# Cumulated sums of the first pair of heads: spread over the partitions by transposes on TensorE, and an exponential ahead

## The chip, the cores and the metric

The kernel runs on one core of a Trainium2 chip. The metric is the time of the device in microseconds (us): the median of three runs before the change is 1105.16 us (1102.88 to 1105.53).

## The reference

Three stages, all in float32 (the weights come as float64 and are converted on the chip):

```python
# q, k, v: (4 batches, 8 heads, 576 positions, 64); f: (4, 8, 576)
scores = q @ k.T / sqrt(64)
cum = cumsum(log(clip(f, 0.0001, 1)), axis=-1)
scores = where(above_diagonal, -1e9, scores + cum[..., :, None] - cum[..., None, :])
attn = softmax(scores) @ v                      # row maximum subtracted first
x = attn as (2304 tokens, 512)
h = x @ w_in; y = max(0.01 * h, h) @ w_out      # 512 -> 2048 -> 512
out = ((y @ w_a) * (y @ w_b)) @ w_o2            # 512 -> 1536 -> 512
```

The term `cum[query] - cum[key]` is the one that the change touches. For a tile with queries on the partitions and keys along the free axis, `cum[query]` is one number per partition, but `cum[key]` is a row that every partition needs: it has to be spread over all 128 partitions.

## The kernel before

The kernel is written in a tile framework. The source says for each instruction which engine it runs on; a planner with its own estimate of every duration then lays out the order on each engine and in each queue, by readiness and priority, and inserts all waits. Priorities: instructions of attention are issued through wrappers (`pe_att`, `act_att`, `dve_att`, `pool_att`) that put them 300 places ahead of others. Each engine works through its instructions strictly in that order. All loads are issued by SP, one queue, in order.

The work is cut into attention blocks (batch b, half r of the queries): block (0, 0) has queries and keys 0 to 255, block (0, 1) the other queries with all keys. A block takes its 8 heads in pairs. For each head `att_scores` makes scores (s, TensorE, into PSUM), the decay tile p (GpSimd: row of sums of the keys, less the sum of the query, then the causal mask by an affine select), adds both and takes the row minimum (VectorE, L330 and its like) and takes the exponential with the row sum (ScalarE, L301). `att_values` transposes p on TensorE (pp), copies it out of PSUM (ph) and multiplies with v (av); a last transpose (px) gives xh, the input of the first dense stage. For batch 0 many instructions show line 76, that of the wrappers.

Beside block (0, 0), and beside the following ones, the weights come in: `fetch_weight` (L115) loads 1 MB of float64 in two requests (raw_a from w_in and from w_out), `convert_weight` turns them into two float32 parts with ScalarE (L94, L87) and VectorE (L95, L96, L97, L100, L88). Weight 1 stands in the order as written, each weight from the third on waits for the beginning of the conversion two before it. The first dense product h (L590) needs all four pairs of block (0, 0) and the first two weights. It is taken 2000 places ahead.

The sums are made at the start (L151 to L166): f is loaded with 32 partitions (one per batch and head), clipped (L152), Ln on ScalarE (L153), a scan on VectorE gives cum (L157), which is written to DRAM as cum_dram (L158). TensorE transposes cum (pc, L162), and ScalarE writes it negated as `ncum_t` (L163) and `ncum_t4` (L165, L166): positions on the partitions, one column per head. In block (0, 0) each pair of heads has a tile cumb of 128 x 2 x 256; it is filled by two DMAs that read a row of cum_dram and repeat it over 128 partitions (L293). In the other blocks each head has its own (L297). The tiles fs, cum and cumb share three slots.

Of the kernel before, what the change touches and what calls it, by code (L numbers as in the profile page):

```python
# [8 lines left out]
F32 = mybir.dt.float32  # L9
# [3 lines left out]
AF = mybir.ActivationFunctionType  # L13
# [4 lines left out]
P = 128  # L18
# [8 lines left out]
def kernel(  # L27
# [13 lines left out]
    nc = tc.nc  # L41
    B, H, S, D = q.shape
# [12 lines left out]
    cum_dram = dram.tile([B * H, S], F32, name="cum_dram")  # L55
# [4 lines left out]
    ident = cpool.tile([P, P], F32, name="ident")  # L60
    make_identity(nc, ident)
    ncum_t = cpool.tile([P, 4, B * H], F32, name="ncum_t")
    ncum_t4 = cpool.tile([P, B * HP], F32, name="ncum_t4")
# [83 lines left out]
    ps_a = att_ctx.enter_context(tc.tile_pool(name="ps_att", bufs=1, space=PSUM, side="right"))  # L147


    fs = ap_.tile([B * H, S], F32, tag="cumb", bufs=3, name="fs")  # L150
    nc.sync.dma_start(fs, f.rearrange("b h s -> (b h) s"))  # L151
    nc.vector.tensor_scalar(fs, fs, 0.0001, 1.0, op0=ALU.max, op1=ALU.min)  # L152
    nc.scalar.activation(fs, fs, AF.Ln)  # L153
    ones = ap_.tile([B * H, S], F32, tag="tk", name="ones")
    nc.vector.memset(ones, 1.0)
    cum = ap_.tile([B * H, S], F32, tag="cumb", bufs=3, name="cum")
# [21 lines left out]
    x4, p4s, stats, qks, xns, vhls, phs, cums, lasts, lastk = ({} for _ in range(10))  # L178

    def att_scores(b, r, h, st):  # L180

        hp, j = h // 2, h % 2
        bh = b * H + h
# [3 lines left out]
        nk = 2 * P if r == 0 else S  # L187
# [101 lines left out]
        if first:  # L289
            if j == 0:  # L290
                cums[hp] = ap_.tile([P, 2, 2 * P], F32, tag="cumb", bufs=3, name=f"cumb_{nm}")
                for u in range(2):
                    nc.sync.dma_start(cums[hp][:, u, :], cum_dram[bh + u : bh + u + 1, :nk].to_broadcast([P, nk]))  # L293
            cumb = cums[hp][:, j, :]
        else:
            cumb = ap_.tile([P, S], F32, tag="cumb", bufs=3, name=f"cumb_{nm}")
            nc.sync.dma_start(cumb[:, :nk], cum_dram[bh : bh + 1, :nk].to_broadcast([P, nk]))  # L297
# [12 lines left out]
        ps = st["ps"] = {}  # L310
        for i in range(2):
            t = 2 * r + i
# [407 lines left out]
    def att_steps(n):  # L720

        if n == 0:

            sts = [{} for _ in range(H)]
            scores = [att_scores(*blocks[n], h, sts[h]) for h in range(H)]
            values = [att_values(*blocks[n], h, sts[h]) for h in range(H)]
            before = None
            for h in range(0, 2):
                next(scores[h])
            for h in range(0, H, 2):  # L730
                for z, _ in enumerate(beside(beside(*scores[h : h + 2]), before)):
                    if z == 3:
                        for g in scores[h + 2 : h + 4]:
                            next(g)
                    yield
                before = chain(*values[h : h + 2])
            yield from before
            return
        second = None
        for h in range(H):  # L740
            st = {}
            yield from beside(att_scores(*blocks[n], h, st), second)
            second = att_values(*blocks[n], h, st)
            if h % 2 == 1 and blocks[n][1] == 1:
                second = chain(second, att_last(blocks[n][0], h // 2, st["rec4"]))
        yield from second
# [143 lines left out]
```

## Time and profile before

| | us |
|---|---|
| median of three runs (lowest, highest) | 1105.16 (1102.88, 1105.53) |
| the profiled execution | 1102.89 |
| its span, first to last instruction | 1101.1 |
| TensorE busy | 1079.5 (98%) |
| VectorE, ScalarE, GpSimd busy | 590.4, 536.7, 224.7 |
| mean granted TensorE clock | 0.992 of full |

The profile shows one execution. PE is TensorE, PEld its loading of weights, DVE is VectorE, ACT is ScalarE, POOL is GpSimd, SPq the queue from which SP issues DMAs. Times are us from the span's start.

### The profile page before, as it was taken

How to read it: one execution, taken by the hardware profiler on the slowest of the kernel's cores; microseconds unless marked ns; L12 is line 12 of the kernel's file. 1: busy time of each engine (PE TensorE's matmuls, PEld its weight loads, DVE VectorE, ACT ScalarE, POOL GpSimd, SP SyncE). 2: the span in 40 equal slices, each digit the busy share in tenths (PEclk: the TensorE clock that was granted, in tenths of full speed). 3: DMA queues.
4: the chain of work that ended last, by engine and by line, in shares of the span. 5: the costliest groups of instructions: out<-in, count | busy, mean ns of one | idle time of the engine just before them, and what ended most of it. 6: DMA issues, size and time to landing. Idle time of an engine off the chain costs nothing.

```text
span 1101.1 us, 19263 instructions
## 1 busy us (share of the span) xinstructions
PE 1079.5 (98%) x7021; PEld 967.4 (88%) x7021; DVE 590.4 (54%) x1314; ACT 536.7 (49%) x1189; POOL 224.7 (20%) x434
## 2 busy tenths in 40 slices
PE   4999999999999999999999999999999999999998
PEld 2768889999999999999999998888888888888897
DVE  5978846787778787677447889212111211211122
ACT  5666657777788777778534565112112111211121
POOL 4734512433233432433000000202001000100000
PEclk9979999999999999999999999999999999999999
DMA  8967225432354233521026562102000100100010
GB/s 232 273 197 203 43 40 107 91 89 47 73 115 81 73 75 74 135 52 48 4 94 195 198 213 93 48 1 77 1 1 20 48 1 1 48 1 1 1 39 20
DMA packets 185727, 86.76 MB, mean 79 GB/s; under 512 B 143840, under 2 KB 173536, under 8 KB 185632
## 3 DMA queue, kind: packets, MB, share of 16 engines
q1 hardware_dynamic: 180736, 80.80, 28.0%
q10 hardware_dynamic: 4896, 4.72, 1.3%
q8 instruction: 56, 0.92, 0.3%
q14 instruction: 39, 0.32, 0.1%
HBM read 75.96 MB, written 9.51 MB: 78 GB/s over the span
## 4 chain that ended last, share of the span: by engine, by line
PE 90%; DMA 4%; issue 1%; DVE 1%; SPq 1%; ACT 1%; POOL 1%; POOLq 0%; DVEq 0%; ACTq 0%
PE ab L686 27%; PE h L590 17%; PE y L617 17%; PE o L709 13%; PE av L76 6%; PE s L76 6%; PE pp L76 4%; DMA raw_a<-in_moe_w_out_dram 1%; DMA cumb<-cum_dram 1%; POOL p L347 0%; DMA vn<-in_v_dram 0%; DMA cum_dram<-cum 0%; DMA xk<-in_k_dram 0%; POOL p L324 0%; SPq L115 0%
## 5 line engine op out<-in xcount | busy, mean ns | idle before, releaser
L686 PE MATMUL ab<-yh,w_ab 128*128 128x512 f32 (+1 forms) x960 | 279.5, 367 | 0.0
L590 PE MATMUL h<-xh,w_a 128*128 128x256 f32 x1152 | 226.9, 283 | 0.5 <-ACT hs L600 0.5
L617 PE MATMUL y<-gh,w_a 128*128 128x256 f32 x1152 | 223.7, 282 | 0.0
L686 PEld LDWEIGHTS ab<-yh,w_ab 128*128 128x128 f32 x960 | 174.2, 188 | 30.4
L692 DVE TENSOR_TENSOR p<-ab,p 128x512 f32<-128x512 f32 (+1 forms) x60 | 38.3, 638 | 285.8 <-PE ab L686 285.8
L590 PEld LDWEIGHTS h<-xh,w_a 128*128 128x128 f32 x1152 | 184.5, 189 | 3.8 <-issue 2.1
L617 PEld LDWEIGHTS y<-gh,w_a 128*128 128x128 f32 x1152 | 182.5, 188 | 2.4 <-issue 1.3
L686 PE MATMUL ab<-yl,w_ab 128*128 128x512 f32 (+1 forms) x480 | 176.2, 367 | 0.0
L590 PE MATMUL h<-xl,w_a 128*128 128x256 f32 x576 | 163.2, 283 | 0.0
L617 PE MATMUL y<-gl,w_a 128*128 128x256 f32 x576 | 161.1, 281 | 0.0
L709 PE MATMUL o<-w_c,pph 128*128 128x512 f32 x432 | 142.5, 389 | 0.0
L691 ACT COPY p<-ab 128x512 f32<-128x512 f32 (+1 forms) x60 | 32.7, 544 | 174.3 <-PE ab L686 174.3
L323 POOL TENSOR_SCALAR p<-cumb,ncum_t 128x384 f32<-128x384 f32 (+1 forms) x112 | 82.8, 747 | 139.7 <-PE pp L76 47.0
L590 PEld LDWEIGHTS h<-xl,w_a 128*128 128x128 f32 x576 | 109.0, 189 | 2.4 <-issue 2.0
L617 PEld LDWEIGHTS y<-gl,w_a 128*128 128x128 f32 x576 | 108.3, 188 | 1.1 <-issue 0.8
L686 PEld LDWEIGHTS ab<-yl,w_ab 128*128 128x128 f32 x480 | 90.1, 188 | 15.3
L88 POOL TENSOR_TENSOR yl<-sy,yh 128x512 fp32r<-128x512 f32 (+1 forms) x16 | 20.0, 1261 | 389.2 <-ACT yh L87 389.0
L87 ACT CAST pph<-p 128x512 fp32r<-128x512 f32 (+1 forms) x60 | 34.6, 578 | 128.4 <-DVE p L692 127.8
L301 ACT ACTIVATE p<-p,stat 128x384 f32<-128x384 f32 (+4 forms) x128 | 76.9, 601 | 39.7 <-DVE stat L330 31.2
L709 PEld LDWEIGHTS o<-w_c,pph 128*128 128x128 f32 x432 | 81.1, 188 | 16.6
L709 PE MATMUL o<-w_c,ppl 128*128 128x512 f32 x216 | 84.2, 390 | 0.0
L602 DVE TENSOR_TENSOR gl<-hs,gh 128x512 fp32r<-128x512 f32 x72 | 51.1, 709 | 40.3 <-ACT hs L600 40.1
(140 smaller groups left out, 1756.9 us busy)
## 6 DMA issues: line engine op xcount, KB each, us to landing
cumb<-cum_dram SPq DMA_DIRECT2D x32, 288.0 KB, 3.7
raw_a<-in_moe_w_in_dram SPq DMA_DIRECT2D x16, 512.0 KB, 4.6
raw_a<-in_moe_w_out_dram SPq DMA_DIRECT2D x16, 512.0 KB, 5.7
raw_ab<-in_moe_w_a_dram SPq DMA_DIRECT2D x12, 512.0 KB, 5.1
raw_ab<-in_moe_w_b_dram SPq DMA_DIRECT2D x12, 512.0 KB, 6.1
raw_c<-in_moe_w_out_dram SPq DMA_DIRECT2D x12, 512.0 KB, 5.7
xq<-in_q_dram SPq DMA_DIRECT2D x144, 32.0 KB, 2.1
y_dram<-yo ACTq DMA_DIRECT2D x18, 256.0 KB, 2.5
```

The costliest lines, as they stand in the source:

```text
L76: return method(*args, **kw)
L87: nc.scalar.copy(hi, src)
L88: (lo_engine or nc.gpsimd).tensor_tensor(out=lo, in0=src, in1=f32(hi), op=ALU.subtract)
L301: act_att.activation(pt, pt, AF.Exp, bias=stat[:, 0, s : s + 1], scale=-1.0, accum_out=stat[:, 1, s : s + 1])
L323: pool_att.tensor_scalar(pt, cumb[:, :n], 1.0, ncum_t[:, t, bh : bh + 1], op0=ALU.mult, op1=ALU.add)
L590: nc.tensor.matmul(hps[:, u, :], w[:, c * P : c * P + P], x[:, c, :], start=(n == 0), stop=(n == 3 * ND - 1))
L602: nc.vector.tensor_tensor(out=gl, in0=hs, in1=f32(gh), op=ALU.subtract)
L617: nc.tensor.matmul(o, w[:, d * P : d * P + P], g[:, u, :], start=(fi == 0 and n == 0 and d % 2 == 0), stop=(fi == NF1 - 1 and n == 2 and d ...
L686: nc.tensor.matmul(o[:, :tn], w[:, c * P : c * P + P], y[:, c, :tn], start=(m == 0), stop=(m == 3 * ND - 1))
L691: nc.scalar.copy(p[:, :tn], ab[0][:, :tn])
L692: nc.vector.tensor_tensor(out=p[:, :tn], in0=ab[1][:, :tn], in1=p[:, :tn], op=ALU.mult)
L709: nc.tensor.matmul(o, g[:, t * P : t * P + P], w, start=(fi == 0 and m == 0), stop=(fi == NF2 - 1 and m == 2))
```

## The change

Two edits. An exponential of one column is issued behind the Ln; its result goes to a place that L165 overwrites later. And in block (0, 0) the first pair of heads no longer fills its cumb by DMA: for each of the two heads and of the two tiles of 128 keys, the column of `ncum_t` is taken as a 128x128 operand that repeats it, and a transpose puts it as a row on all 128 partitions of a PSUM tile rep (128 x 512 in all); ScalarE copies that, times -1, to cumb. cum_dram is written as before, and the other three pairs and all other blocks read it as before. `nc.tensor` and `nc.scalar` are the engines without the 300 places of the wrappers.

```diff
@@ -151,6 +151,7 @@
     nc.scalar.activation(fs, fs, AF.Ln)
+    nc.scalar.activation(ncum_t4[0 : B * H, 0:1], fs[:, 0:1], AF.Exp)
     ones = ap_.tile([B * H, S], F32, tag="tk", name="ones")
@@ -289,8 +290,15 @@
         if first:
             if j == 0:
                 cums[hp] = ap_.tile([P, 2, 2 * P], F32, tag="cumb", bufs=3, name=f"cumb_{nm}")
-                for u in range(2):
-                    nc.sync.dma_start(cums[hp][:, u, :], cum_dram[bh + u : bh + u + 1, :nk].to_broadcast([P, nk]))
+                if hp == 0:
+                    rep = ps_a.tile([P, 2, 2, P], F32, tag="ps", bufs=3, name="rep")
+                    for u in range(2):
+                        for t in range(2):
+                            nc.tensor.transpose(rep[:, u, t, :], ncum_t[:, t, bh + u : bh + u + 1].to_broadcast([P, P]), ident)
+                    nc.scalar.mul(cums[hp], rep.rearrange("p u t k -> p u (t k)"), -1.0)
+                else:
+                    for u in range(2):
+                        nc.sync.dma_start(cums[hp][:, u, :], cum_dram[bh + u : bh + u + 1, :nk].to_broadcast([P, nk]))
             cumb = cums[hp][:, j, :]
```

## Rows read from the trace of the kernel before

**Rows 1.** Busy time by stretch: stretch, us; PE, PEld, DVE, ACT, POOL; clock, DMA, GB/s.
```profile
0.00:25.00 25.00, 11.01 (x35) 6.01 (x35) 13.89 (x27) 12.24 (x26) 9.98 (x24) 1.00 0.78 220
16.00:20.00 4.00, 2.33 (x6) 1.00 (x4) 1.27 (x5) 2.07 (x4) 3.77 (x11) 1.00 1.05 392
25.00:61.00 36.00, 34.45 (x126) 24.12 (x125) 35.83 (x77) 25.13 (x52) 27.60 (x32) 0.90 0.93 268
54.50:70.90 16.40, 15.09 (x46) 8.79 (x46) 13.14 (x27) 9.68 (x19) 5.85 (x7) 0.50 0.83 232
61.00:68.60 7.60, 6.42 (x16) 2.82 (x15) 4.38 (x11) 2.96 (x7) 0.98 (x2) 0.50 0.86 249
72.00:1101.00 1029.00, 1024.17 (x6831) 931.10 (x6830) 533.64 (x1199) 494.23 (x1101) 183.89 (x376) 1.00 0.26 67
```

**Rows 2.** The chain of waits, 5 to 19 us: start, us, what.
```profile
5.36 3.98 DMA cum_dram<-cum
...
11.64 7.28 DMA raw_a<-in_moe_w_out_dram
```

**Rows 3.** Timeline, 3 to 17 us: start, us, instruction, count, idle of its engine before.
```profile
3.27 0.68 ACT L153 ACTIVATE fs<-fs 32x576 f32<-32x576 f32 x1 [1.25 <-DVE fs L152]
4.95 0.38 ACT L76 ACTIVATE qn<-tqk 128x256 f32<-128x256 f32 x1 [0.99 <-PE tqk L76]
6.01 0.69 PE L76 MATMUL tqk<-ident,xk 128*128 128x128 f32 x2
6.12 0.28 ACT L163 ACTIVATE ncum_t<-pc 128x128 f32<-128x128 f32 x1 [0.78 <-PE pc L162]
7.29 0.80 PE L76 MATMUL s<-kn,qn 64*128 64x128 f32 x4 [0.59 <-DVE kn L76]
8.83 1.12 ACT L94 ACTIVATE c_a<-raw_a 128x1024 f32<-128x1024 f32 x1 [2.19 <-DMA raw_a<-in_moe_w_out_dram]
12.43 2.32 POOL L76 TENSOR_SCALAR p<-cumb,ncum_t 128x128 f32<-128x128 f32 x3 [11.11 <-DMA cumb<-cum_dram]
15.29 1.28 ACT L76 ACT_TABLE_LOAD   x1
16.59 0.40 ACT L76 ACTIVATE p<-p,stat 128x128 f32<-128x128 f32 x1
```

**Rows 4.** Prices: PE's group, 29 to 32 us; a page's group; POOL's tiles (min/median/max ns).
```profile
L76 PE MATMUL pp<-ident,p 128*128 128x128 f32 x6 | 1.5, 421 | 0.0
L691 ACT COPY p<-ab 128x512 f32<-128x512 f32 (+1 forms) x60 | 32.7, 544 | 174.3 <-PE ab L686 174.3
L76 POOL TENSOR_SCALAR p<-cumb,ncum_t x12: 370/478/2048, 12.4 to 27.9; 128x128 f32<-128x128 f32 x6, 128x256 f32<-128x256 f32 x6
L76 POOL TENSOR_SCALAR_AFFINE_SELECT p<-p x8: 291/292/294, 14.7 to 19.5; 128x128 f32<-128x128 f32 x8
```

**Rows 5.** Timeline of VectorE, 9 to 15 us: the first of five instructions and the last.
```profile
9.98 0.69 DVE L95 TENSOR_SCALAR c_a<-c_a 128x1024 f32<-128x1024 f32 x1 [2.75 <-ACT c_a L94]
...
12.92 1.22 DVE L100 SCALAR_TENSOR_TENSOR c_a<-raw_a,c_a 128x1024 int32<-128x1024 int32 x1
```

**Rows 6.** Timeline of SP's queue, 9 to 18 us.
```profile
9.36 1.76 SPq L293 DMA_DIRECT2D cumb<-cum_dram  x4
11.17 0.42 SPq L115 DMA_DIRECT2D raw_a<-in_moe_w_in_dram  x1
...
15.88 2.09 SPq L293 DMA_DIRECT2D cumb<-cum_dram  x2
```

**Rows 7.** Groups of VectorE, 20 to 30 us: count, busy us, mean ns, idle before.
```profile
L76 DVE CUSTOM_DVE_ANT_0 p<-s,p 128x256 f32<-128x256 f32 x3 | 1.2, 414 | 0.0
...
L76 DVE CUSTOM_DVE_ANT_0 p<-s,p 128x128 f32<-128x128 f32 x2 | 0.5, 284 | 0.0
L76 DVE DVE_READ_ACCUMULATOR2_ANT stat<- 128x1 f32 x5 | 0.4, 81 | 0.0
L76 DVE TENSOR_SCALAR rec<-stat 128x4 f32<-128x4 f32 x1 | 0.4, 372 | 0.0
```

## The prediction

> **What bounds the kernel now.** I read the busy time by stretch first, then the chain of waits, then the timelines of the first 25 us. From 72 us to the end TensorE is busy for 1024.17 of 1029 us [rows 1]: whatever comes there earlier moves the end one for one. In the first 25 us it is busy for 11.01 us only, so 14.0 us are idle, three times what is left behind 72 us (4.83). The question is how much sooner the front, ahead of 72 us, hands over.
>
> The front has another pace-maker. Between 25 and 61 us VectorE is busy for 35.83 of 36 us, the DMA engines for 0.93 of the time [rows 1]: VectorE carries both the softmax and the conversion of the weights, and has no hole left. Ahead of that it has holes, 11.1 us in the first 25 and 2.73 of them in the four from 16 to 20.
>
> The chain of waits says what made them. The write of the cumulated sums to DRAM holds the chain from 5.36 to 9.34 us; then SP issues four copies back from there, and only behind these the second weight, which lands 7.28 us after its last issue, at 18.9 [rows 2].
>
> **The change part by part.** *The early exponential.* The Ln on ScalarE ends at 3.27 + 0.68 = 3.95 us. Now a table load of 1.28 us stands at 15.29, ahead of the first exponential at 16.59 [rows 3]. It will stand behind the Ln, to 5.23; the one-column exponential costs no more than the 0.28 us of the first write of the negated sums, so ScalarE is free at 5.5. The scaling of q (0.38), which starts at 4.95, slips by 0.55 and ends at 5.9; what may wait for it, the transposes of k, starts at 6.01 on TensorE [rows 3]. So it costs nothing, with 0.1 us of cover; without that, 0.55 us at most. Its gain, 1.28 us for the first exponential, is part of the lead below.
>
> *The four transposes and their eviction.* They need the negated sums, written at 6.12 + 0.28 = 6.40 us, and TensorE, which is through with k at 6.70 [rows 3]. Six 128x128 transposes in a row take 1.5 us, so four take 1.0; four lone ones, at the mean of 421 ns, would take 1.7 [rows 4]; the lower end is not below nothing, as nothing is taken out of TensorE. I take 1.0, since they are issued back to back: 6.7 to 7.7. The scores, now at 7.29 after 0.59 idle us, follow to 8.5, before anything needs them. In a full stretch the transposes would cost their 1.0 us. The eviction of 128x512 takes 0.54 us by the row of the same shape [rows 4] and ends at 8.3, inside the 2.19 idle us that ScalarE has ahead of the first weight at 8.83 [rows 3]. The transposes also take a PSUM slot of three; the next user is the transpose of p behind the first exponential, long after, so no wait.
>
> *What starts sooner.* GpSimd's first tile of p waits 11.11 us, to 12.43, for the copies from DRAM [rows 3]. It can now start at 8.3: a lead of 4.1 us, 3.4 with the dear transposes. VectorE's first reduce follows some 0.7 us later (0.37 and 0.29 on GpSimd, [rows 4]), ahead of the first conversion at 9.98 [rows 5], and the first exponential near 9.5 us instead of 16.59. What is late next is pair 1: its copies still come through DRAM, behind 9.34 us.
>
> *What SP no longer issues.* Four copies take 1.76 us from 9.36; two go, 0.88 us [rows 6]. The second weight (11.17) goes out 0.88 us sooner, and so does all else on that queue. The write of the sums stays, and so does the wait on it, now at the head of pair 1's copies. The two copies are 256 KB; at the 392 GB/s of 16 to 20 us [rows 1] that is 0.65 us of traffic, which I count below only against the DMA engines' limit.
>
> **The sum.** (a) The conversions of the second weight start 0.88 us sooner. (b) Between 20 and 30 us, among the conversions, VectorE does five softmax reduces of pairs 0 and 1 with their reads and the addition to a row sum: 1.2 + 0.5 + 0.4 + 0.4 = 2.5 us [rows 7]. With pair 0 four us ahead, and GpSimd with it, most of these fit in the 2.73 idle us of 16 to 20. Lower end nothing, upper end 2.5; I take all but one 128x256 reduce with its read (0.41 + 0.08), 2.0 us, since pair 1's last tile also has to come through GpSimd. (c) From 25 us on VectorE, 2.9 us ahead, runs into the DMA engines: their slack is 0.07 of 36 us, 2.5 us, and the 0.65 us saved make up the rest. No deduction. So the front hands over 2.9 us sooner.
>
> The profiled execution took 1102.89 us, 1.8 more than its span; less 2.9, 1100.0. It lies 2.27 us below the median of the runs, 1105.16, so in the median's terms the forecast is **1102.3 us**. With the ends of (a) and (b), and 0.65 us for the traffic on top, the gain runs from 0.9 to 4.0 us: 1101.2 to 1104.3.
>
> **A row and a rule against it.** One kind of instruction on GpSimd takes 0.37 us at best and 2.05 at worst [rows 4]. The dear one is the first, at 12.43 [rows 3]; all that time VectorE runs conversions, the last of them from 12.92 to 14.14 with two inputs [rows 5]. The Trainium skill ("SBUF — State Buffer", Who interferes with whom) says that VectorE and GpSimd share one pair of ports under an exclusive lock, and that an instruction of GpSimd that reads stands still for the whole of a VectorE instruction with two inputs in SBUF. The trace agrees (2.05 against 0.37 us). By that rule pair 0's later tiles, which now meet the first weight's conversion, would wait it out, and the gain would be that of the first rival, 1.6 us, instead of 2.9.
>
> **The rivals.** *The lead is lost behind the conversion* (chance 0.19). GpSimd gets two 128x128 tiles done before 9.98 us and the rest only behind 14.14, as now. For it: the 2.05 us of [rows 4]. Against it: between 9.98 and 14.14 four times one instruction of VectorE ends and the next begins [rows 5], where GpSimd can get in. Then (b) is two 128x128 reduces with reads, 2 x (0.28 + 0.08) = 0.7, and with (a) the gain is 1.6: 1103.6.
>
> *The whole lead carries, and more* (0.22). From 54.5 to 70.9 us the granted clock is half, 1.2 GHz; within that, from 61 to 68.6, VectorE is busy for only 4.38 of 7.6 us [rows 1], so TensorE is the bound there, at half its speed. If 4.1 us of that stretch's work are done before 54.5, at full clock, and the dense products that end it start sooner, I estimate 1 us on top of the lead (a third of the 3.2 us that VectorE idles): 5.1, 1100.1. Against it: pair 1, the weights and the DMA engines do not get the lead.
>
> *Slower* (0.13). The order is laid out anew by the planner's own estimates. With pair 0 early its buffers come free sooner, and the planner can put the copies of pair 2 ahead of the second weight on SP. These stand at 15.88 and take 2.09 us, to 17.97, instead of 0.88, because SP waits there [rows 6]. A weight that goes out behind them, at 17.97 instead of 11.17, is 6.8 us late, and VectorE, which has nothing else by then, loses that in full: less the 2.9 gained, 3.9 us slower, 1109.1. It decides from a slip of 2.9 us, an issue at 14.1. Against it: weight 1 is held in the order written.
>
> *The load doesn't move* (0.06). If the one-column exponential comes out behind the scaling and the copies on ScalarE, the table load lands in front of the eviction and costs the lead 1.28 us; with (b) cut by as much the gain is 1.6, 1103.6.
>
> **How the numbers follow.** The forecast has 0.40, its own range 1100.6 to 1104.3. About 0.3%, 3.3 us, is what a measurement of this kernel tells from no change; the bound, 1101.85, lies just under the forecast. Faster: half of the forecast (0.20), all of the carried lead (0.22) and 0.01 of the unmoved load, 0.43. Slower: 0.09 of the slower rival (the whole slip) and 0.02 of the lost lead, if the transposes land in a full stretch as well, 0.11. Within: the rest, 0.46. The range 1098.8 to 1106.4 leaves out the top of the slower rival (0.09) and the far ends of the carried and of the lost lead (0.09).
>
> **What would show it.** One table load behind the Ln, ending near 5.3, none near 15; four transposes between 6.4 and 8.5; GpSimd's first tile at 8 to 9 us and the first exponential near 10; two copies from DRAM behind 9.34 instead of four, and the second weight's issue near 10.3; VectorE without a hole from 19 us; the stretch at half clock ended, and TensorE full, near 68 us instead of 71. The prediction is wrong if these come and TensorE is no sooner full, if the weights' issues slip, or if the stretch at half clock grows.

## The result, and the profile after

The change made the kernel slower. Median of six runs: 1102.87 us before, 1111.12 us after (1110.18 to 1112.31); the ratio is 1.0064, 95% interval [1.0046, 1.0083]. The forecast was 1102.3 us, 0.9974 of the 1105.16 that it started from. The profiled execution took 1110.23 us, its span is 1108.4. In the experiments below the kernel before ran beside each group, with medians from 1102.5 to 1105.9 us, so kernels are compared by the recorded ratio to it, which stands behind each median and is not the quotient of two medians.

Busy time by stretch, of the kernel after, as in [rows 1]:
```profile
0.00:25.00 25.00, 17.75 (x63) 11.62 (x63) 15.96 (x37) 15.81 (x35) 11.48 (x25) 1.00 0.76 209
16.00:20.00 4.00, 3.94 (x14) 2.77 (x13) 2.90 (x11) 2.89 (x9) 1.46 (x2) 1.00 1.08 363
25.00:61.00 36.00, 28.75 (x99) 18.17 (x97) 32.49 (x67) 20.80 (x45) 21.75 (x30) 0.56 0.89 261
61.00:68.60 7.60, 7.60 (x18) 2.95 (x17) 5.34 (x10) 3.93 (x9) 3.51 (x3) 0.50 0.91 266
72.00:1108.40 1036.40, 1028.15 (x6835) 934.22 (x6834) 530.43 (x1199) 493.26 (x1102) 182.59 (x378) 1.00 0.26 67
```
The start is fuller, as meant: TensorE is busy for 17.75 of the first 25 us instead of 11.01, VectorE for 2.90 of the four from 16 to 20 instead of 1.27. Between 25 and 61 us the lead turns round: VectorE now has 3.5 idle us where it had 0.17. And behind 72 us TensorE idles 8.25 us instead of 4.83, in a stretch that is 7.4 us longer.

The timeline of the start, of the kernel after, as in [rows 3, 6] (start, us, instruction, count, idle before):
```profile
3.92 1.28 ACT L154 ACT_TABLE_LOAD   x1
5.22 0.20 ACT L154 ACTIVATE ncum_t<-fs 32x1 f32<-32x1 f32 x1
5.33 0.36 ACT L76 ACTIVATE qn<-tqk 128x256 f32<-128x256 f32 x1
6.43 1.08 PE L297 MATMUL rep<-ident,ncum_t 128*128 128x128 f32 x4
...
7.55 0.60 ACT L298 ACTIVATE cumb<-rep 128x512 f32<-128x512 f32 x1 [0.96 <-PE rep L297]
8.24 1.63 POOL L76 TENSOR_SCALAR p<-cumb,ncum_t 128x128 f32<-128x128 f32 x4 [6.93 <-ACT cumb L298]
9.41 0.81 SPq L301 DMA_DIRECT2D cumb<-cum_dram  x2
9.83 1.97 POOL L76 TENSOR_SCALAR_AFFINE_SELECT p<-p 128x128 f32<-128x128 f32 x4
10.27 0.42 SPq L115 DMA_DIRECT2D raw_a<-in_moe_w_in_dram  x1
10.63 0.28 DVE L76 CUSTOM_DVE_ANT_0 p<-s,p 128x128 f32<-128x128 f32 x1
10.95 0.40 ACT L76 ACTIVATE p<-p,stat 128x128 f32<-128x128 f32 x1
...
13.59 1.21 DVE L100 SCALAR_TENSOR_TENSOR c_a<-raw_a,c_a 128x1024 int32<-128x1024 int32 x1
14.18 1.32 POOL L76 TENSOR_SCALAR p<-cumb,ncum_t 128x128 f32<-128x128 f32 x2 [0.49 <-DMA cumb<-cum_dram]
```
Every small step came within a few tenths of the forecast: the load behind the Ln, 1.08 us of transposes (1.0), an eviction of 0.60 (0.54), GpSimd at 8.24 (8.3), the second weight's issue at 10.27 (10.3). Only the first exponential came at 10.95 instead of 9.5: GpSimd made all four tiles ahead of its first select (9.83), and the reduce ran behind the first instruction of the conversion, not ahead of it. So the question is not whether the change works but where its lead went.

Who ScalarE waited for, 20 to 70 us: first the kernel before, then the kernel after (us in total, times, longest):
```profile
ACT c_a L94 <- DMA raw_a<-in_moe_w_out_dram: 2.8, 2, 1.9
```
```profile
ACT c_a L94 <- DMA raw_a<-in_moe_w_out_dram: 11.8, 5, 4.0
```
The conversions wait for weights: the load of the sixth, for one, goes out at 39.10 us instead of 34.27, with 13 copies of q, k, v and the sums between the fifth and it on SP instead of 10. The planner laid the whole program out anew. Take the old and the new order of each queue for the same work and count the places at which they hold different instructions: on VectorE 632 of 1146 places differ, on TensorE 3123 of 6877, from the 18th to the 4101st.

Who TensorE waited for, 75 to 480 us: the kernel before, then the kernel after:
```profile
PE h L590 <- ACT hs L600: 0.5, 1, 0.5
...
PE s L76 <- DVE stat L330: 0.2, 1, 0.2
...
```
```profile
PE s L76 <- DVE stat L338: 1.9, 3, 1.1
PE h L598 <- ACT hs L608: 1.5, 3, 0.6
...
```
The longest of these waits lie at 175, 207, 243 and 446 us, at least 160 us behind the four transposes, in instructions that the change does not touch.

### The profile page after: what moved, and what is told of

Read it like the earlier page. It is cut to its first block, busy times and chain, and to the rows that moved or that the text cites. A ratio compares the mean times of both kernels' runs of the same rounds, so it can differ in the third digit from the quotient of the medians.

```text
span 1108.4 us, 19265 instructions
## 1 busy us (share of the span) xinstructions
PE 1085.7 (98%) x7025; PEld 970.4 (88%) x7025; DVE 587.5 (53%) x1314; ACT 535.3 (48%) x1191; POOL 219.3 (20%) x434
## 4 chain that ended last, share of the span: by engine, by line
PE 86%; DMA 5%; DVE 3%; ACT 2%; issue 2%; SPq 1%; POOL 1%; POOLq 0%; DVEq 0%; ACTq 0%
PE ab L694 27%; PE h L598 16%; PE y L625 15%; PE o L717 13%; PE s L76 6%; PE av L76 5%; PE pp L76 3%; DMA raw_a<-in_moe_w_out_dram 2%; DMA cumb<-cum_dram 1%; DMA xq<-in_q_dram 1%; ACT p L348 1%; DVE ks L281 0%; DVE p L338 0%; DMA y_dram<-yo 0%; PE tk L76 0%
## 5 line engine op out<-in xcount | busy, mean ns | idle before, releaser
L625 PE MATMUL y<-gh,w_a 128*128 128x256 f32 x1152 | 227.1, 283 | 0.0
L331 POOL TENSOR_SCALAR p<-cumb,ncum_t 128x384 f32<-128x384 f32 (+1 forms) x112 | 74.6, 674 | 138.4 <-PE pp L76 59.1
```

Of the source, the lines that this page charges most:

```text
L331: pool_att.tensor_scalar(pt, cumb[:, :n], 1.0, ncum_t[:, t, bh : bh + 1], op0=ALU.mult, op1=ALU.add)
L625: nc.tensor.matmul(o, w[:, d * P : d * P + P], g[:, u, :], start=(fi == 0 and n == 0 and d % 2 == 0), stop=(fi == NF1 - 1 and n == 2 and d ...
```

## The experiments

All but the first two carry the order of one of the two kernels, or a splice of both, written out. To the program one function is added (shortened here); it puts each instruction behind the one ahead of it in a list, queue by queue, without a wait, so that the planner has nothing left to choose:

```diff
+def pin(tc):
+    for queue, order in PLAN.items():
+        for a, b in zip(order, order[1:]):
+            tc.add_manual_dep(traced[queue][b], traced[queue][a].name, NO_WAIT, reason="pin")
...
     tile_decay_attention__moe__moe2_kernel(tc, *args)
+    pin(tc)
```

"Old order" is that of the kernel before, "new order" that of the kernel after. By their medians seven runs lie outside every range that was expected of them (the exponential alone, the change in the old order, old front with new rest, new to 314 us, N = 3, and the two with early spare matmuls); the theories are told apart by the ratios.

### Order or work: four runs

The first two need no list; each has one of the change's two edits (the diff stands above).

**The exponential alone.** Expected:

> The kernel before with the early exponential alone. On all queues but ScalarE's the order of the work stays that of the kernel before. Theory A (the loss comes from the new order that the planner gives the whole program once the transposes are in): no loss here, 1101 to 1103.5 us, and the table load of 1.28 us gone from its place at 15.3. Theory B (the loss comes from the work that was added or from the clock): 1102 to 1104 as well, since the one exponential is too small to cost 8 us. Above 1106 would speak against both.

Measured: 1105.3 us, ratio 1.0011 [0.9996, 1.0027].

**The transposes alone.** Expected:

> The change without the early exponential: transposes and their eviction only. The queues of TensorE, VectorE, GpSimd and SP hold exactly the order of the changed kernel. Theory A: 1109 to 1112, with the table load back ahead of the first exponential, which alone costs at most 1.3. Theory B: the same if it is the transposes' work, their PSUM slot or the clock that costs; if it were the early exponential, 1102 to 1104.

Measured: 1110.87 us, 1.0062 [1.0045, 1.0079].

**The change in the old order.** `+ PLAN = old order; the exponential behind the Ln, rep behind k's transposes, its eviction behind ncum_t4`. Expected:

> The whole change, with the order of the kernel before written out on every queue (the four transposes behind those of k, the eviction behind the negated sums, the exponential behind the logarithm). Theory A: at or below the kernel before, 1099 to 1103, with the second weight 0.9 us earlier and the milestones behind 170 us as in the kernel before or earlier. Theory B: 1109 to 1112, as the changed kernel, because it does the same work at the same places.

Measured: 1104.53 us, 1.0005 [0.9987, 1.0022].

**The kernel before in the new order.** `+ PLAN = new order; pair 0's two copies ahead of pair 1's`. Expected:

> The work of the kernel before (trip through DRAM, late exponential) in the order of the changed kernel on every queue. Theory A: 1108 to 1114, as slow as the changed kernel or slower, as the order counts on rows of sums that are not there yet. Theory B: 1101 to 1104, as the kernel before.

Measured: 1110.23 us, 1.0060 [1.0041, 1.0078].

TensorE's waits of the last two, 75 to 480 us, first the change in the old order, then the kernel before in the new one:
```profile
PE h L598 <- ACT hs L608: 0.5, 1, 0.5
PE s L76 <- DVE stat L338: 0.3, 1, 0.3
PE s L76 <- DVE st L379: 0.2, 1, 0.2
```
```profile
PE h L590 <- ACT hs L600: 3.0, 3, 1.9
PE s L76 <- DVE stat L330: 1.3, 2, 0.7
...
```
The waits go with the order, not with the work, and so does the time: the loss stands without a single instruction of the change (1.0060), and with all of them none is left that the runs can tell (1.0005). The transposes cause it, but only by making the planner lay out another order. Of the change's own gain little is left: in its profiled execution the first dense matmul starts at 67.69 instead of 68.63 us and the span is 0.9 shorter (1100.2), which the runs cannot tell from nothing.

### Where in the order: five runs

`+ PLAN = one order up to a point, the other behind it`, always with the change's work, and a control of the writing out itself.

**Old to the first dense matmul, then new.** Expected:

> The change, with the old order written out up to the first dense matmul (68 us) and the new order from there on. At 75 us the changed kernel had 1.9 us more matmul work left than the kernel before; behind 75 us it had 3.2 us more idle time on TensorE and 2.0 us dearer matmuls. Theory R (most of the loss lies in the order of the rest): 1106 to 1108, with idle time behind 75 us near 4.3 us, as in the changed kernel. Theory F (the front's order makes the loss and the rest only inherits it): 1101 to 1104, with some 1.1 us idle behind 75 us.

Measured: 1111.47 us, 1.0050 [1.0032, 1.0068].

**New to the first dense matmul, then old.** Expected:

> The change, with the new order up to the first dense matmul and the old order from there on. Theory R: 1102 to 1105, that is at most the 1.9 us by which the new front was behind at 75 us, the clock's late rise included. Theory F: 1107 to 1111.

Measured: 1104.11 us, 0.9993 [0.9981, 1.0006].

**Old to 314 us, then new.** Expected:

> The change, with the old order up to the end of the third block of the first expert layer (314 us) and the new order from there on. By 314 us the changed kernel was 7.2 us late and at the end 7.3. Theory R as the traces have it: the order behind 314 us costs at most 1.2 us (the idle time that stands there), so 1100 to 1104. If the order behind 314 us costs more than that, 1105 or more, the lateness at 314 us was only borrowed.

Measured: 1110.08 us, 1.0033 [1.0014, 1.0051].

**New to 314 us, then old** (run with the next group). Expected:

> The change, with the new order up to the end of the third block of the first expert layer (314 us) and the old order from there on. The new order up to 68 us cost nothing measurable and the new order behind 314 us cost 3.7 us of the 5.5 that the whole rest costs. If the parts add up: 1104 to 1107, some 2 to 3 us above the same order's old rest, with the waits at 208 and 243 us and none at 330 or 458. If the loss needs the whole new order (a late queue that carries lateness on from the front), it is either none (1102 to 1105) or all of it (1109 or more).

Measured: 1108.8 us, 1.0032 [1.0020, 1.0044].

**Control: the kernel before, its own order written out.** Expected:

> The kernel before with its own order written out on every queue, as a control: both theories expect the same time as the kernel before, 1101 to 1105, and the same trace. A second profile of this order also shows where TensorE's granted clock rises in another execution.

Measured: 1104.08 us, 0.9990 [0.9977, 1.0004]: writing an order out costs nothing that shows.

The new front, with its late weights, costs nothing that shows. The rest costs 5.5 us (0.50% of 1105.9 us). The two pieces that meet at 314 us cost 0.32% and 0.33%, each within some 0.2%: both lose, and their sum is near the loss of the kernel after (0.64%). My reading ahead of the third run, at most 1.2 us behind 314 us, was wrong: I had taken the lateness of block marks at 314 us (7.2 us) for the loss up to there, but in another order another amount of work stands ahead of such a mark.

A better account is by work. For each run I took what is left behind 75 us, each form of matmul by its mean price in the kernel before; how much more the same matmuls took than that; and TensorE's idle time. All three are worked out from the records of TensorE in one profiled execution each, in us, as differences to the kernel before but for the idle time:

| run | work left at 75 us | dearer behind it | idle behind it |
|---|---|---|---|
| before | 0 | 0 | 1.1 |
| after | +1.9 | +2.0 | 4.3 |
| before, new order | +2.0 | +2.1 | 5.2 |
| change, old order | -0.6 | -0.6 | 1.1 |
| old front, new rest | +0.5 | +3.8 | 5.2 |
| new front, old rest | +0.8 | -0.6 | 1.0 |

For the kernel after: 1.9 + 2.0 + 3.2 = 7.1 of the 7.3 us by which its span is longer. The three runs with the new rest are 2 to 4 us dearer there and idle 3 to 4 us more, whatever front they have. What makes the same matmuls dearer stays open; in the run with old front and new rest an estimated 1.7 of the 3.8 us come from 3.4 us at half clock, shown in the last section.

### Which wait, which queue: three runs

In the run with old front and new rest TensorE's longest wait is at 458 us. Its timeline (start, us, instruction, idle before):
```profile
449.97 1.05 ACT L633 COPY yo<-y 128x512 f32<-128x512 f32 x2
451.61 0.39 ACTq L634 DMA_DIRECT2D y_dram<-yo  x1
457.33 0.60 ACT L608 ACTIVATE hs<-h 128x512 f32<-128x512 f32 x1 [2.60 <-DMA y_dram<-yo]
457.98 0.38 PE L598 MATMUL h<-xh,w_a 128*128 128x256 f32 x1 [1.74 <-ACT hs L608]
```
hs and yo share two slots. In the new order both yo are evicted together, and their copies to DRAM leave 0.49 us apart (3.79 in the kernel before), among loads of q and k as before; they take twice as long. The copies of that stretch (queue, KB, median us to landing), before and in this run:
```profile
y_dram<-yo ACTq DMA_DIRECT2D x2, 256.0 KB, 2.8
```
```profile
y_dram<-yo ACTq DMA_DIRECT2D x2, 256.0 KB, 5.8
```
In the kernel after, hs waits 0.87 us at this place and TensorE 0.3; the kernel before in the new order has it at full size (2.69 and 1.9). So what follows weighs a wait of the new rest that the kernel after itself has only in small.

Is that wait a cause, or only where lateness shows? The two copies were to leave one block later. In each run block N's sums are left out, and those of block N + 1 are written in both places, so the transfers stay as many (shortened):

```diff
-                nc.scalar.dma_start(y_dram[..., i * T1 : i * T1 + T1]..., yo)
+                for n in () if i == N else (N, N + 1) if i == N + 1 else (i,):
+                    nc.scalar.dma_start(y_dram[..., n * T1 : n * T1 + T1]..., yo)
```

**N = 3.** Expected:

> Old order up to the first dense matmul and new order behind it (the run that took 1111.5), but the two copies of the fourth block's sums to DRAM leave with those of the fifth block (so that block's tokens get wrong sums; all other work is done). Theory Y: at 458 us TensorE idles 1.74 us because ScalarE's hs waits 2.60 us for the slot that these copies hold for 5.7 us, and the granted clock falls to half for 3.4 us right behind: without them the idle time at 458 falls below 0.3 us and the half-clock stretch goes: 1108 to 1110, 1.5 to 3.4 us less. Rival: the place is only where lateness shows, and another wait takes its place: 1111 to 1112.

Measured: 1114.7 us, 1.0097 [1.0075, 1.0118]. I had miscounted: the copies at 452 us are those of N = 4. This run took away the copies at 381 us and sent four instead of two at 452. So it raised the suspected cost, and these are its waits, 449 to 459 us:
```profile
ACT xn L499 <- DMA y_dram<-yo: 4.2, 1, 4.2
PE av L76 <- DVE rec L315: 3.0, 1, 3.0
```
ScalarE stood 4.2 us at the copies' issue instead of 2.6 at hs, and TensorE 3.0 us instead of 1.7.

**N = 4.** Expected:

> Old order up to the first dense matmul and new order behind it (1111.5), with the two copies that leave at 452 us held back until the next block's leave at 515 us (the block they belong to gets wrong sums). In the earlier run with this aim the wrong block was taken: four copies instead of two left at 452 us, and TensorE's idle time there grew from 1.74 to 3.03 us. Theory Y: with none there, hs no longer waits 2.6 us, the idle time at 458 us is below 0.3 us, and the time is 1108 to 1110.5. Rival: another wait takes its place, 1111 to 1112.5.

Measured: 1110.02 us, 1.0037 [1.0021, 1.0053]. The wait is gone, no wait of TensorE above 0.3 us takes its place there, and the median is 1.5 us below that of the order with both copies in place. A worse wait there costs time: 1.0097 against 1.0050, intervals apart (the 381 us copies, taken away in the same run, are not told apart from it). That its removal gives time back isn't settled: 1.0037 against 1.0050, intervals overlapping. By the medians it would be 1.5 of 5.5 us.

**SP and GpSimd in the old order behind the first dense matmul, the other three in the new one.** Expected:

> Old order up to the first dense matmul; behind it SP and GpSimd keep the old order as well, and only TensorE, VectorE and ScalarE take the new one. Theory D (the new order of the copies on SP, sums and q and k behind each other, and of GpSimd's tiles feeds the attention late): 1104 to 1107. Theory E (the loss comes from how the compute engines' own queues are laced): 1110 to 1113, as with all queues in the new order.

Measured: 1112.27 us, 1.0048 [1.0031, 1.0065]. TensorE's waits, 75 to 480 us:
```profile
PE s L76 <- DVE stat L338: 3.2, 4, 1.3
PE h L598 <- ACT hs L608: 2.7, 3, 1.5
```
Putting the copies and GpSimd's tiles back in the old order gives nothing back. That speaks for how TensorE, VectorE and ScalarE are laced, but doesn't show it alone: the mixture has waits of its own (3.2 us for stat, against 1.2 with all queues in the new order). Which pieces stand badly, beyond the one at 458 us, stays open; no run exchanged one of those three queues by itself.

### The half clock of the front: six runs

The control's profile showed something else. Granted clock by stretch (as in [rows 1], the clock is the last but two): the kernel before, then the same order in the control:
```profile
50.70:54.00 3.30, 2.79 (x14) 1.44 (x12) 3.30 (x4) 1.84 (x3) 2.35 (x3) 1.00 1.02 331
54.20:68.60 14.40, 13.09 (x37) 6.79 (x37) 11.18 (x25) 7.79 (x15) 4.17 (x5) 0.50 0.85 238
68.60:71.10 2.50, 2.50 (x13) 2.50 (x12) 2.46 (x3) 2.09 (x4) 1.88 (x2) 0.50 0.81 227
71.20:80.00 8.80, 8.80 (x70) 7.73 (x69) 6.54 (x15) 5.48 (x10) 3.20 (x4) 1.00 0.45 138
```
```profile
46.50:61.00 14.50, 13.98 (x47) 9.39 (x47) 12.83 (x25) 7.53 (x15) 6.10 (x7) 0.50 0.96 260
71.00:76.80 5.80, 5.72 (x27) 5.72 (x27) 3.31 (x4) 2.15 (x5) 2.28 (x2) 0.50 0.79 230
77.00:90.00 13.00, 13.00 (x95) 10.78 (x95) 11.82 (x23) 8.33 (x15) 2.91 (x3) 1.00 0.47 156
```
The control has no full stretch near 50 us (its short one is at 32.5 to 35.8); its first dense matmul comes at 71.63 instead of 68.63, and the clock is full 5.2 us behind that instead of 2.5. Its span is 4.0 us longer, with the same order. And the "1.00" at the start does not fit the durations: I read it as what stands there until the first change is recorded. The same pair of score matmuls, in the kernel before at "1.00", and in the kernel after in its full stretch (26 to 29 us) and at 0.50:
```profile
25.30 1.22 PE L76 MATMUL s<-kn,qn 64*128 64x256 f32 x2
```
```profile
28.35 0.70 PE L76 MATMUL s<-kn,qn 64*128 64x256 f32 x2 [1.51 <-DVE stat L76]
39.13 1.22 PE L76 MATMUL s<-kn,qn 64*128 64x256 f32 x2
```
So the front runs at half clock, 1.2 GHz, but for stretches such as 50.7 to 54 us in the kernel before and 26 to 29 us in the kernel after. Does that swallow the lead? Spare matmuls that nobody reads keep TensorE busier, at places in its old order, with a PSUM slot that is free there. Each shows as two records in the trace. The late ones, here 25 (early ones are written likewise, to another slot):

```diff
+    hot = ps_y.tile([P, 512], F32, tag="y", bufs=2, name="hot")
+    for _ in range(25):
+        nc.tensor.matmul(hot[:, 0:P], ident, ident, start=True, stop=True)
```

**16 in the holes of the first 25 us, 25 from 35 us on.** Expected:

> The change in the old order, with 16 spare 128x128 matmuls in TensorE's holes of the first 25 us and 25 more, one behind every third instruction from 35 us to the first dense matmul (nothing reads them). Theory C: the front runs at half clock nearly all the time, and in executions without a full stretch at 50 us the first dense matmul comes 3 us later and the clock rises 5 us behind it: with TensorE kept busier the clock is full earlier, 1098 to 1102 and less spread. Rival: at half clock the spare matmuls take 0.43 us each of a TensorE that is busy for 32.6 of 36 us: 10 us more work on the path, 1105 to 1112.

Measured: 1102.86 us, 0.9985 [0.9969, 1.0001].

**16 and 36.** Expected:

> As the run with 25 spare matmuls, with 36 of them, one behind every second instruction. Theory C: full clock for more of the front, 1096 to 1102. Rival: 5 us more than with 25, 1108 to 1117.

Measured: 1105.35 us, 1.0018 [0.9999, 1.0037].

**25 from 35 us on.** Expected:

> The change in the old order with the 25 spare matmuls from 35 us on, and none in the holes of the first 25 us. With both, the clock rose at 46.5 us and was full when the dense matmuls began, but the first transposed tile came at 32.62 instead of 30.49 us. Theory C: the late ones alone bring the clock, and the 2.1 us come back: 1099 to 1102. Rival: the early ones were needed for the rise: 1104 to 1108, with the dense matmuls at half clock.

Measured: 1100.38 us, 0.9962 [0.9943, 0.9981].

**18 from 35 us on.** Expected:

> As the run with 25 late spare matmuls, with 18, one behind every fourth instruction. Theory C: 1099 to 1103. Rival: too few for the clock, 1103 to 1107.

Measured: 1100.1 us, 0.9951 [0.9935, 0.9967], against 1105.94 for the kernel before on the same chip.

**The kernel before with 18.** Expected:

> The kernel before, in its own order, with the 18 late spare matmuls (nothing reads them): what do they bring without the change? The change in the old order with these 18 took 1100.1, the change in the old order without them 1104.5, beside the kernel before at 1102.5 to 1105.9. Theory C (the spare matmuls bring the whole gain through the clock, the change at most the 0.9 us by which its front was ahead): 1099.5 to 1102.5. Rival (the gain needs the change's lead): 1103 to 1106.

Measured: 1101.31 us, 0.9976 [0.9959, 0.9993].

**The kernel after, new order, with 17.** Expected:

> The changed kernel in its own new order with 17 late spare matmuls, one behind every fourth instruction. Theory C and order together: the front's half clock is mended and some 3 to 5 us come back, the order's waits behind 75 us stay: 1105 to 1108, with 3 us or more of idle time behind 75 us. If the half clock was all of the loss: 1100 to 1102. If the clock had no part in it: 1110 to 1112.

Measured: 1107.96 us, 1.0042 [1.0018, 1.0065].

The run with 25 from 35 us on, two of its spare matmuls, its stretches, and its first dense matmul beside that of the kernel before:
```profile
45.10 0.79 PE L801 MATMUL hot<-ident 128*128 128x128 f32 x2
46.52 0.44 PE L801 MATMUL hot<-ident 128*128 128x128 f32 x2
46.50:61.00 14.50, 12.92 (x87) 9.82 (x87) 14.27 (x29) 10.51 (x23) 8.16 (x9) 1.00 1.00 267
61.00:66.50 5.50, 4.46 (x21) 2.45 (x20) 4.70 (x11) 2.76 (x6) 1.49 (x2) 1.00 0.58 140
66.57 0.36 PE L598 MATMUL h<-xh,w_a 128*128 128x256 f32 x1
```
```profile
68.63 0.56 PE L590 MATMUL h<-xh,w_a 128*128 128x256 f32 x1
```
A spare matmul (x2) falls from 0.79 to 0.44 us: the clock is full from 46 us. It does not fall again, and the dense matmuls start 2.1 us earlier and at full speed (0.9 of the 2.1 the change in the old order has without them). The early 16 bring nothing that shows: 0.9985 with them against 0.9962 without, intervals overlapping.

Eighteen late ones have the lowest ratio here, faster than the kernels before and after; from 25 the runs can't tell them. In their profiled execution, the slowest of its five (1102.44 us), the clock was at half again from 53.4 to 63.7 us and the dense matmuls began at 69.08, so no trace shows where its faster executions gain. The kernel before with 18 does show it: behind 50 us the clock is at half for 3.4 us instead of 17.1, and its dense matmuls begin at 66.5 instead of 68.63.

The kernel before gains 0.24% by them, and the change in the old order with them lies 0.49% below the kernel before without them; so the change may be worth a quarter of a per cent once the clock is mended, but these two intervals overlap, and it isn't settled. In the new order 17 do not mend the front: in the profiled execution one of them still takes 0.63 us at 64.3 and 0.39 only at 68.5. The run keeps 4.1 us of idle time and 1.9 us of dearer matmuls behind 75 us, and its interval overlaps that of the kernel after (1.0042 and 1.0064).

## Why the prediction was wrong, point by point

**The step that failed** is the premise of the first paragraph, "whatever comes there earlier moves the end one for one": it takes the order of the work behind 72 us as given. The four transposes made the planner write another order, and behind 75 us that one idles 3.2 us more and pays 2.0 us more for the same matmuls, with 1.9 us more of them left to do. The kernel before in that order loses as much (1.0060) as the change does (1.0064). In the old order the two traces fit the premise (dense matmuls 0.94 us earlier, span 0.9 shorter).

**A second step failed with it**, the size of the lead. The sum gave 2.9 us, a ratio of 0.9974; in the old order, where nothing is lost behind 75 us, the change has 1.0005 [0.9987, 1.0022].

**The sum.** Term (a), 0.88 us from SP, came: 0.90 at the second weight's issue (10.27 against 11.17). Term (b), 2.0 us of reduces moved ahead of 20 us, came in the new order only: VectorE has done seven by then instead of three, four more, 1.7 us of work with their reads, all ahead of 16 us. It was not a gain. The conversion of the second weight began 1.07 us earlier (17.93 against 19.00), but the fourth weight, which waits for that, went out 0.93 us later (23.25 against 22.32), behind copies of q, k and the sums on SP; ScalarE waits 11.8 us for weights instead of 2.8. "No deduction" for (c) failed: the dense matmuls started 0.42 us earlier instead of 2.9, at half clock for 5.5 us instead of 2.5. The recorded range also begins at 1100.6, below the 1101.2 that the sum's own ends give, without a reason.

**The exponential and the transposes** cost nothing of themselves that shows, as forecast: 1.0011 for the first, 1.0005 for all the work in the old order.

**The row and the rule.** GpSimd's first four tiles took 1.63 us together, with no conversion on VectorE beside them. The four selects from 9.83, beside instructions of the conversion with one input each (L95, L96), took 1.97, against four at 0.29 [rows 4]. Two tiles at 14.18, beside the one with two inputs (L100) that ends at 14.80, took 1.32, against 0.8 for two of the first four. The Trainium skill ("SBUF — State Buffer", Who interferes with whom) says of a VectorE instruction with two inputs in SBUF that it contends with a GpSimd instruction that reads there; the trace agrees at 14.18. That is 1.3 us of GpSimd's time in all, not the lead, and the first rival's price of 1.3 us less gain does not reach the loss either.

**The slower rival** had the right culprit at the wrong place. I let the planner reorder one queue in the front, SP, with a price of 3.9 us and a chance of 0.13. The second weight kept its place, as I said there; the front's other slips cost nothing measurable (0.9993). The order that costs is that of the rest, and with SP and GpSimd put back there the loss stays (1.0048).

**The carried lead and the half clock.** I read "1.00" in [rows 1] as full clock up to 54.5 us. The durations say half, but for 50.7 to 54. So the 1 us for work done ahead of 54.5 us "at full clock" had no ground. What a fuller clock is worth is read from the spare matmuls: 2.6 us off the kernel before (0.24%), and with the change in the old order 5.4 us (0.49%).

## What to carry to other kernels

Where a planner lays the order out, price the order apart from the work: run the change in the old order and the old work in the new one, before any mechanism is looked for. If the second alone is as slow as the change, keep the old order, and judge the change in that. And before a stretch's granted clock is used, check it against the duration of one form of matmul in it.

## What the runs showed of the hardware that was not expected

Executions of one program differ by the clock of the front. Of 23 of the kernel before, beside the last runs, seven with a mean granted clock of 0.984 to 0.986 took 1101.7 to 1103.8 us, and nine with 0.981 took 1106.0 to 1107.7; the other seven fit neither group. The control's profiled execution (0.981, 1106.9) belongs to the second. That of the kernel before has the time of the first (1102.9), with 0.992. The mean is a poor guide, as the time before the first recorded change counts as full: of the other seven, two with 0.998 took 1097.3 and 1100.9 us, and four with 0.999 or 1.0 took 1104.5 to 1106.9. With the 18 spare matmuls the twelve executions of the kernel before lie between 1100.1 and 1103.7.

In the run with old front and new rest the clock fell once more in full work, right behind the idle 1.74 us at 458:
```profile
450.00:458.00 8.00, 6.19 (x49) 5.96 (x49) 4.11 (x14) 4.33 (x14) 3.70 (x9) 1.00 0.59 138
458.30:461.60 3.30, 3.30 (x18) 3.30 (x17) 2.44 (x9) 2.70 (x9) 0.31 (x1) 0.50 0.49 105
461.80:470.00 8.20, 8.20 (x71) 8.20 (x71) 3.61 (x11) 4.91 (x13) 1.56 (x5) 1.00 0.50 112
```
By my estimate these 3.3 us at half clock cost half of themselves, nearly as much again as the wait. The wait alone does not bring the fall: the kernel before in the new order idles 1.87 us at the same place, and the run with N = 3 3.03 us, and both stay at 1.00 there. What decides is open.
